# Two more input blocks in one pass, weight parts moved by transfers, and a new order behind the first 200 entries

## The chip, the cores and the metric

The kernel runs on one core of a Trainium2 chip. The metric is the device time of one execution in microseconds; smaller is better. TensorE does the matmuls into PSUM, VectorE, ScalarE and POOL (GpSimd) work elementwise, and SyncE's queue issues most of the transfers (DMA).

## The reference

Four batches of a chunked state-space recurrence (8 heads, 768 steps, head size 32, state size 16) are followed by a two-layer network with SiLU:

```
for c in range(nc):                                  # chunks of 32 steps
    cum = np.cumsum(log_a[:, :, sl], axis=-1)
    L = np.exp(cum[..., :, None] - cum[..., None, :]) * causal
    M = np.einsum('bhin,bhjn->bhij', Cc, Bc) * L
    y[:, :, sl] = M @ xc  +  einsum(Cc, state) * exp(cum)
    state = exp(sum(la)) * state + sum(Bx over the chunk)
x = y as [3072, 256]
h = x @ w_in            # [256, 2048]
g = h * 1 / (1 + exp(-h))
out = g @ w_out         # [2048, 256]
```

## The kernel before

**Tiling.** The 3072 rows are 12 units of 256 steps (unit u, three to a batch) and six pairs G of units, so a pair has 512 rows. W_in and W_out each come as eight blocks of 256 hidden columns (weights n = 0 to 7 are W_in, 8 to 15 are W_out). The weights arrive as 64-bit values and are turned into fp32 by bit operations: `lw` loads, `u` and `v` on ScalarE, `w` on VectorE, `W` on POOL.

**Two ways to multiply.** A plain fp32 matmul is recorded as two passes and is slow. The other way splits each operand into three fp32r parts, high `h`, low `l` and third `d`, and multiplies part with like part, in one pass each ("one-pass" below): three quick matmuls for one product. Pairs 1 to 5 go this way wholly. Pair 0 goes one-pass for W_in blocks 6 and 7; blocks 0 to 5 are plain fp32 (`s`, L697), and so is its whole second layer (`n1`, L761).

**The order** is written out by hand in one string, `SCHEDULE`, of 1309 entries. Each entry issues one step, and every engine and queue takes its instructions in that order. A second table, `SLOTS`, names the place of each buffer, in the order of allocation. So when a place is free again follows from these two. The entries used below:

- state part of unit u: `Lt`, `La`, `Ln`, `Lx`, `Lp` loads (SyncE); `T` transposition, `E` scans, `M` masks, `S` state steps (VectorE, L525, L512, L600, L615); `ce`, `b`, `SM`, `y`, `xh` (ScalarE; `b` is L594, `SM` L623); `B`, `C` (POOL); `g0`, `gd`, `Y` matmuls (L585, L571, L635 and L644); `x,u,0` and `x,u,1` the low and third part of the unit's output (VectorE, L651, L654)
- first layer, pair 0, plain: `s,u,j` four fp32 matmuls of 256 columns, `si` SiLU on ScalarE (L703)
- first layer, one-pass: `a,G,i` eight matmuls (high and low parts), `ax` a rescaling on ScalarE (L811), `d,G,i` four matmuls (third part), `dg` SiLU (L821); then `h` (ScalarE, L827), `l` (VectorE, L651) and `e` (VectorE, L837) split the result
- second layer: `n1,f,m` (pair 0, one fp32 matmul), `q,P,i,k,m` (three one-pass matmuls, L782), then `Va`, `Vd`, `o`, `O` for the output
- parts of weight block n: `H` high (ScalarE, L322); `lD` low and `dD` third (VectorE, L326, L330); or in their place, for W_out, `Wl` and `Wd`, which copy the scaled high part on ScalarE (L335), and `Wm` and `We`, which add the rest in place by an accumulating transfer that POOL issues (L339)

Before, W_out blocks 12 to 15 have both parts by `Wl`/`Wm` and `Wd`/`We`, blocks 10 and 11 the low part alone, and blocks 8 and 9 both parts on VectorE (`lD`, `dD`).

**What stands around the change.** On TensorE, `a,G,i` writes one of two PSUM tiles, `ga` (even i) or `gb` (odd i), which the state part uses too; `d` follows when `ax` has rescaled the tile. A unit's `Y` needs `SM` and `M`, and these need `gd` and `g0`.

Of the kernel before, what the change touches and what calls it, by code (L numbers as in the profile page):

```python
# [39 lines left out]
n1,2,0 W,11 H,10 a,1,0 Wl,10 Wm,10 n1,3,1 n1,4,0 Lt,4,1,2,0 T,4,1 x,3,1 si,1,3 S,3,3 Lp,4,0 C,4 ce,4,1 E,4,0 H,11 ax,1,0  # L40
d,1,0 E,4,1 ce,4,0 Lt,4,0,2,0 n1,5,1 Wl,11 Lx,5,1,0 Wl,13 dg,1,0 n1,4,1 T,4,0 H,8 lD,1 Ln,4,0,0,0 g0,4 lD,2 Ln,4,0,1,0
B,4 H,9 M,4,1 La,5,1,0 Wm,11 Lx,4,1,0 Wm,12 gd,4 b,4,0 lD,8 b,4,1 dD,1 n1,6,1 h,1,0 S,4,0 S,4,1 Lx,5,0,0 H,3 S,4,2
SM,4,1 n1,14,0 n1,6,0 SM,4,0 Lt,5,1,3,0 M,4,0 n1,7,0 Vn,0 Y,4 y,4,1 y,4,0 xh,4 l,1,0 n1,7,1 S,4,3 a,1,2 Vn,1 lD,9 dD,8
dD,2 H,5 a,1,1 ax,1,2 e,1,0 q,1,0,1,0 d,1,2 dD,9 q,1,0,0,1 Ln,5,0,0,0 ax,1,1 d,1,1 Wd,13 Lt,5,1,1,0 q,1,0,0,0 q,1,0,1,1
AD,3 Lt,5,1,0,0 dD,4 dg,1,2 Lt,5,0,3,0 h,1,2 a,1,4 dg,1,1 h,1,1 Lt,5,1,2,0 T,5,1 ce,5,0 Lt,5,0,2,0 ce,5,1 Lt,5,0,0,0
lD,3 a,1,3 Lp,6,0 dD,10 o,0,1,2 We,12 dD,3 x,4,1 x,4,0 l,1,2 e,1,2 ax,1,4 d,1,4 H,14 q,1,2,0,1 Ln,5,0,1,0 ax,1,3 d,1,3
l,1,1 La,5,0,0 E,5,0 dg,1,4 e,1,1 q,1,1,1,1 dg,1,3 Lt,5,0,1,0 h,1,3 q,1,1,0,1 E,5,1 T,5,0 g0,5 B,5 M,5,1 Lp,5,0 C,5 gd,5
b,5,1 lD,5 Lt,6,1,0,0 b,5,0 S,5,0 Lt,6,1,3,0 S,5,1 Wm,13 We,13 dD,5 q,1,2,1,1 La,6,0,0 q,1,2,0,0 a,1,5 Lx,6,1,0 Wl,14
ax,1,5 M,5,0 q,1,1,1,0 l,1,3 S,5,2 q,1,1,0,0 SM,5,1 dD,11 La,6,1,0 e,1,3 SM,5,0 d,1,5 h,1,4 dg,1,5 h,1,5 o,0,0,2
Lt,6,1,2,0 Lt,6,1,1,0 T,6,1 q,1,2,1,0 l,1,4 e,1,4 q,1,3,0,0 l,1,5 e,1,5 q,1,3,1,0 Wd,15 Y,5 E,6,1 Lt,6,0,1,0 y,5,0 y,5,1  # L50
xh,5 q,1,3,1,1 q,1,3,0,1 ce,6,0 Lt,6,0,0,0 a,1,7 ce,6,1 q,1,4,0,0 q,1,5,1,0 Lt,6,0,3,0 ax,1,7 q,1,4,1,0 Lt,7,1,1,0 Wm,15
We,15 d,1,7 q,1,4,1,1 dg,1,7 Lt,6,0,2,0 Wd,14 q,1,5,1,1 E,6,0 q,1,5,0,1 T,6,0 h,1,7 g0,6 Ln,6,0,1,0 x,5,0 Lx,6,0,0
Ln,6,0,0,0 B,6 La,7,1,0 M,6,1 gd,6 b,6,1 Lt,7,1,0,0 x,5,1 Wm,14 M,6,0 q,1,4,0,1 a,2,1 b,6,0 ax,2,1 a,1,6 ax,1,6 S,6,0
S,6,1 Lt,7,0,0,0 C,6 S,6,2 l,1,7 e,1,7 SM,6,1 S,6,3 d,2,1 dg,2,1 SM,6,0 q,1,7,1,0 We,14 d,1,6 dg,1,6 h,1,6 q,1,5,0,0
Lt,7,1,2,0 q,1,7,0,0 Lt,7,1,3,0 T,7,1 ce,7,1 q,1,7,0,1 Lt,8,1,1,0 Y,6 Ln,7,0,1,0 q,1,7,1,1 y,6,0 h,2,1 l,1,6 e,1,6 a,2,0
ax,2,0 q,1,6,1,0 l,2,1 e,2,1 q,1,6,1,1 y,6,1 xh,6 O,0,1,2,0,0 q,1,6,0,1 Va,1,1 x,6,1 q,1,6,0,0 d,2,0 dg,2,0 a,2,3 x,6,0
La,7,0,0 E,7,1 a,2,2 E,7,0 Va,1,0 Vd,1,0 h,2,0 l,2,0 Ln,7,0,0,0 B,7 O,0,0,2,1,0 Lp,8,0 ce,7,0 ax,2,3 q,2,1,1,0 Lx,7,1,0
d,2,3 q,2,1,0,0 Lt,7,0,3,0 Vd,1,1 Ln,8,0,0,0 ax,2,2 d,2,2 e,2,0 q,2,0,1,1 q,2,0,0,0 dg,2,3 dg,2,2 Lx,7,0,0 Lt,7,0,1,0
Lt,7,0,2,0 T,7,0 h,2,3 l,2,3 g0,7 gd,7 b,7,0 Lt,8,0,2,0 q,2,0,1,0 q,2,1,1,1 M,7,1 e,2,3 q,2,0,0,1 o,1,0,2 q,2,1,0,1
Lt,8,1,3,0 a,2,5 q,2,3,1,1 Lp,7,0 b,7,1 o,1,1,2 O,1,1,2,2,0 S,7,0 S,7,1 ax,2,5 S,7,2 O,1,0,2,3,0 Lx,8,0,0 M,7,0  # L60
q,2,3,1,0 h,2,2 SM,7,0 S,7,3 O,0,0,2,2,0 La,8,0,0 Lt,8,0,0,0 a,2,4 l,2,2 SM,7,1 ax,2,4 Lt,8,1,0,0 d,2,5 dg,2,5 h,2,5
q,2,3,0,0 d,2,4 C,7 dg,2,4 h,2,4 e,2,2 q,2,3,0,1 q,2,2,1,0 q,2,2,1,1 Lt,8,1,2,0 T,8,1 ce,8,1 O,0,1,2,3,0 ce,8,0 Y,7
y,7,0 O,1,1,2,3,0 y,7,1 q,2,2,0,0 l,2,4 e,2,4 a,2,6 l,2,5 a,2,7 O,0,1,2,1,0 O,1,1,2,0,0 e,2,5 Lx,8,1,0 Lt,8,0,1,0
# [64 lines left out]
def kernel(  # L128
# [82 lines left out]
    def f32(t):  # L211
        return t.bitcast(FP32)
# [61 lines left out]
    WF = 256  # L274
# [614 lines left out]
```

## Time and profile before

| what | value |
|---|---|
| median of 3 runs | 329.56 us (329.25 to 329.67) |
| the profiled execution's own time | 329.1 us |
| its span in the profile | 327.4 us |
| mean granted clock of TensorE | 0.999 |
| TensorE matmul records | 3064 |
| L782 (second layer, one-pass) | 400 + 80 records, 110.0 + 30.7 us busy |
| L800 (first layer, one-pass) | 504 records |
| L697 (first layer, pair 0, plain) | 96 records, 22.3 us busy |
| L761 (second layer, pair 0, plain) | 64 records, 30.0 us busy |
| transfers | 29.27 MB |

Busy times are unions over records and are given with their share of the span. A group row has line, engine, operation, output and inputs, shape, count, then busy time, the mean of one in ns, and the idle time of the engine just before with what ended it. In the chain of waits a piece has its start, its length, and the work; "x8" are eight records.

### The profile page before, as it was taken

What the parts mean: (1) busy time and instruction counts of PE and PEld (TensorE: products, weight loads), DVE (VectorE), ACT (ScalarE), POOL (GpSimd) and SP (SyncE); (2) the same over time, 40 slices, a digit from 0 to 9 for tenths busy, and PEclk for the clock granted to TensorE, in tenths of its full rate; (3) what the DMA queues carried; (4) which work ended last, traced back from release to release, by engine and by line L of the source; (5) the groups of instructions that cost most, each with busy time, mean ns of one, the idle gap of its engine ahead of it and who ended that gap; (6) DMA issues with size and microseconds to landing.
All of it is one profiled execution on the core that took longest, in us unless ns stands there. A gap on an engine that the chain in (4) does not pass through costs nothing.

```text
span 327.4 us, 7519 instructions
## 1 busy us (share of the span) xinstructions
PE 320.3 (98%) x3064; PEld 243.4 (74%) x3067; DVE 240.4 (73%) x331; ACT 209.5 (64%) x319; POOL 56.0 (17%) x74
## 2 busy tenths in 40 slices
PE   8999999999999999999999999999999999999994
PEld 3478576655687777878887778878887788888883
DVE  4998999999988965877687299665787544635553
ACT  4679978648696846583771875837775455574641
POOL 1364766326102330001200010010001000000000
PEclk9999999999999999999999999999999999999999
DMA  6979966479872663423633306514042000050003
GB/s 162 206 200 272 296 175 192 51 148 135 148 127 46 105 115 53 86 36 64 147 74 70 44 1 117 104 26 96 3 74 37 7 2 2 0 88 0 2 1 64
DMA packets 94962, 29.27 MB, mean 89 GB/s; under 512 B 80000, under 2 KB 86912, under 8 KB 94928
## 3 DMA queue, kind: packets, MB, share of 16 engines
q1 hardware_dynamic: 90960, 25.71, 37.5%
q0 software_dynamic: 1616, 2.82, 5.1%
q10 hardware_dynamic: 2352, 0.26, 0.6%
q8 instruction: 24, 0.39, 0.5%
q14 instruction: 10, 0.08, 0.1%
HBM read 22.81 MB, written 3.34 MB: 80 GB/s over the span
## 4 chain that ended last, share of the span: by engine, by line
PE 94%; SPq 2%; DMA 1%; DVE 1%; issue 1%; DVEq 0%
PE hp L782 29%; PE ga L800 18%; PE gb L800 18%; PE hp L761 9%; PE hp L697 6%; PE o_ps L782 6%; PE ga L635 2%; PE ga L585 2%; PE ga L644 2%; DMA s2k<-in_C_dram 1%; PE gb L644 1%; PE ga L571 1%; SPq L262 0%; SPq L375 0%; PE o_ps L531 0%
## 5 line engine op out<-in xcount | busy, mean ns | idle before, releaser
L782 PE MATMUL hp<-r4k,s2k 128*128 128x512 f32 x400 | 110.0, 394 | 0.0
L651 DVE SCALAR_TENSOR_TENSOR r4k<-r4k,r4k 128x1024 fp32r<-128x1024 f32 (+1 forms) x42 | 50.5, 1202 | 51.3 <-ACT r4k L827 48.2
L782 PEld LDWEIGHTS hp<-r4k,s2k 128*128 128x128 f32 x400 | 74.0, 188 | 16.4 <-issue 0.3
L800 PE MATMUL ga<-raw,s2k 128*128 128x512 f32 x240 | 62.3, 395 | 0.0
L800 PE MATMUL gb<-raw,s2k 128*128 128x512 f32 x240 | 61.1, 390 | 0.0
L800 PEld LDWEIGHTS ga<-raw,s2k 128*128 128x128 f32 x240 | 44.7, 188 | 11.4 <-ACT ga L811 0.9
L800 PEld LDWEIGHTS gb<-raw,s2k 128*128 128x128 f32 x240 | 44.8, 188 | 9.9 <-ACT gb L811 0.5
L837 DVE SCALAR_TENSOR_TENSOR r4k<-r4k,r4k 128x1024 fp32r<-128x1024 f32 x40 | 49.2, 1231 | 3.4 <-DVE r4k L651 0.9
L827 ACT ACTIVATE r4k<-r4k 128x1024 fp32r<-128x1024 f32 x40 | 42.2, 1058 | 3.2 <-issue 1.3
L811 ACT ACTIVATE ga<-ga 128x1024 f32<-128x1024 f32 x21 | 21.1, 1007 | 24.6 <-PE ga L800 23.8
L811 ACT ACTIVATE gb<-gb 128x1024 f32<-128x1024 f32 x21 | 21.2, 1009 | 17.6 <-PE gb L800 13.3
L782 PE MATMUL o_ps<-r4k,s2k 128*128 128x512 f32 x80 | 30.7, 390 | 0.0
L761 PE MATMUL hp<-r4k,s2k 128*128 128x512 f32 x64 | 30.0, 602 | 0.0
L821 ACT ACTIVATE r4k<-gb 128x1024 f32<-128x1024 f32 x21 | 21.4, 1021 | 12.4 <-PE gb L800 9.9
L520 POOL TENSOR_TENSOR BT<-bn,ab 128x256 f32<-128x256 f32 x10 | 6.7, 672 | 129.5 <-DVE ab L512 123.3
L318 POOL TENSOR_TENSOR s2k<-s2k,s2k 128x512 uint32<-128x512 uint32 (+1 forms) x19 | 23.6, 1250 | 26.4 <-DVE s2k L307 13.7
L821 ACT ACTIVATE r4k<-ga 128x1024 f32<-128x1024 f32 x21 | 21.5, 1023 | 8.4 <-PE ga L800 8.2
L512 DVE TENSOR_TENSOR_SCAN ab<-ab,diag 128x512 f32<-128x512 f32 x20 | 24.8, 1265 | 0.0
L697 PE MATMUL hp<-r4k,s2k 128*128 128x256 f32 x96 | 22.3, 382 | 0.2 <-issue 0.2
L697 PEld LDWEIGHTS hp<-r4k,s2k 128*128 128x128 f32 x96 | 18.0, 190 | 4.0 <-issue 1.4
L761 PEld LDWEIGHTS hp<-r4k,s2k 128*128 128x128 f32 x64 | 11.6, 189 | 10.5 <-issue 9.6
L782 PEld LDWEIGHTS o_ps<-r4k,s2k 128*128 128x128 f32 x80 | 15.0, 188 | 3.2
(123 smaller groups left out, 384.8 us busy)
## 6 DMA issues: line engine op xcount, KB each, us to landing
ab<-az SPq DMA_DIRECT2D x20, 256.0 KB, 4.2
raw<-in_moe_w_in_dram SPq DMA_DIRECT2D x8, 512.0 KB, 4.2
raw<-in_moe_w_out_dram SPq DMA_DIRECT2D x8, 512.0 KB, 8.0
out_dram<-r4k SPq DMA_DIRECT2D x44, 64.0 KB, 2.0
xt<-in_x_dram SPq DMA_DIRECT2D x20, 128.0 KB, 4.2
s2k<-s2k POOLq DMA_DIRECT2D x10, 256.0 KB, 3.8
pfx<-ac SPq DMA_DIRECT2D x10, 130.0 KB
bn<-in_B_dram SPq DMA_DIRECT2D x20, 64.0 KB, 5.2
```

Of the source, the lines that this page charges most:

```text
L318: nc.gpsimd.tensor_tensor(out=u[:, :, fs], in0=u[:, :, fs], in1=v[:, :, fs], op=ALU.add)
L512: nc.vector.tensor_tensor_scan(out=o, data0=src, data1=diag.rearrange("p h t -> p (h t)"), initial=0.0, op0=ALU.mult, op1=ALU.add)
L644: nc.tensor.matmul(out=y[w][32 * q:32 * q + 32, c, 64 * k:64 * k + 64], lhsT=xc[64 * c:64 * c + 64, k, h], rhs=m[64 * c:64 * c + 64, k, h] ...
L651: nc.vector.scalar_tensor_tensor(out=l, in0=f32(h), scalar=BACK, in1=y, op0=ALU.mult, op1=ALU.add)
L697: nc.tensor.matmul(out=hp[:, i], lhsT=WT[j][:, kc, 128 * i:128 * i + 128], rhs=XM()[:, 2 * kc:2 * kc + 2, u], start=(kc == 0), stop=(kc == ...
L761: nc.tensor.matmul(out=NP[m], lhsT=WT[8 + f // 2][:, f % 2, 128 * m:128 * m + 128], rhs=GT[0, f // 2][:, f % 2], start=(n == 1), stop=(n = ...
L782: nc.tensor.matmul(out=ACC[P, c], lhsT=WK[8 + i, p][:, k, 128 * m:128 * m + 128], rhs={"h": HT, "l": LT, "d": DT}[p][P, i][:, k], start=(n ...
L800: nc.tensor.matmul(out=o, lhsT=WK[j, q][:, kc, 128 * i:128 * i + 128], rhs=xs[:, 2 * kc:2 * kc + 2], start=(start and q == "h" and kc == 0 ...
L811: nc.scalar.activation(t, t, AF.Copy, scale=1.0 + Z)
L821: nc.scalar.activation(g, t, AF.Silu, scale=BACK)
L827: nc.scalar.activation(t, GT[G, i], AF.Copy, scale=-LESS * Z)
L837: nc.vector.scalar_tensor_tensor(out=DT[G, i], in0=f32(HT[G, i]), scalar=-1.0, in1=f32(LT[G, i]), op0=ALU.mult, op1=ALU.subtract)
```

## The change

- W_in blocks 2 and 3 ("three, four") of pair 0 go one-pass: `s,u,2`, `s,u,3` and their `si` (u = 0, 1) are gone; `a`, `ax`, `d`, `dg` for `0,2` and `0,3` come. They use parts of x that exist for blocks 6 and 7 already, and parts of W_in that pairs 1 to 5 use as well, so these are made earlier.
- A new step `Wc` copies the high part of a W_out block to the place of its low part by a transfer on SyncE's queue. It takes the place of `Wl` for blocks 10 to 15 and, with `Wm`, that of `lD` for blocks 8 and 9. Their third parts come by `Wd` and `We` in the place of `dD`.
- The first 200 entries of `SCHEDULE` are kept. The 1113 behind them, and the places in `SLOTS`, stand in another order. Two more steps (`ds`, `dl`) are defined and not used.

The entries that are gone and that came:

```
gone:  s,0,2 s,1,2 s,0,3 s,1,3  si,0,2 si,1,2 si,0,3 si,1,3  lD,8 dD,8 lD,9 dD,9
       Wl,10 Wl,11 Wl,12 Wl,13 Wl,14 Wl,15
came:  a,0,2 ax,0,2 d,0,2 dg,0,2  a,0,3 ax,0,3 d,0,3 dg,0,3
       Wc,8 Wc,9 Wc,10 Wc,11 Wc,12 Wc,13 Wc,14 Wc,15  Wm,8 Wm,9  Wd,8 Wd,9 We,8 We,9
```

The core of the diff, with the stretch of the order around unit 4 and the entries around block 14 and at the end:

```diff
+    def w_copy(n):
+        t = WK[n, "l"] = small(f"l{n}", [128, 2, WF], FR)
+        nc.sync.dma_start(out=f32(t).rearrange("p k f -> p (k f)"), in_=f32(WK[n, "h"]).rearrange("p k f -> p (k f)"))
...
-        "Wl": lambda n: w_part(n, "l"), "Wd": lambda n: w_part(n, "d"), "Wm": lambda n: w_more(n, "l"),
+        "Wl": lambda n: w_part(n, "l"), "Wd": lambda n: w_part(n, "d"), "Wc": w_copy, "Wm": lambda n: w_more(n, "l"),
...
-B,4 H,9 M,4,1 La,5,1,0 Wm,11 Lx,4,1,0 Wm,12 gd,4 b,4,0 lD,8 b,4,1 dD,1 n1,6,1 h,1,0 S,4,0 S,4,1 Lx,5,0,0 H,3 S,4,2
-SM,4,1 n1,14,0 n1,6,0 SM,4,0 Lt,5,1,3,0 M,4,0 n1,7,0 Vn,0 Y,4 y,4,1 y,4,0 xh,4 l,1,0 n1,7,1 S,4,3 a,1,2 Vn,1 lD,9 dD,8
...
-Ln,6,0,0,0 B,6 La,7,1,0 M,6,1 gd,6 b,6,1 Lt,7,1,0,0 x,5,1 Wm,14 M,6,0 q,1,4,0,1 a,2,1 b,6,0 ax,2,1 a,1,6 ax,1,6 S,6,0
-S,6,1 Lt,7,0,0,0 C,6 S,6,2 l,1,7 e,1,7 SM,6,1 S,6,3 d,2,1 dg,2,1 SM,6,0 q,1,7,1,0 We,14 d,1,6 dg,1,6 h,1,6 q,1,5,0,0
...
+Wc,12 E,4,0 Lt,4,0,2,0 Lt,4,0,1,0 T,4,0 g0,4 Ln,4,0,1,0 B,4 gd,4 n1,3,1 La,5,0,0 n1,5,1 b,4,0 lD,1 M,4,1 S,4,0 b,4,1
+S,4,1 S,4,2 Wc,9 Lx,5,1,0 SM,4,1 M,4,0 C,4 SM,4,0 Y,4 Lt,5,1,3,0 n1,6,1 Vn,0 Lt,5,0,1,0 y,4,0 dD,1 y,4,1 Vn,1 xh,4 Wc,10
...
+h,1,3 Wc,15 B,5 q,1,2,1,1 g0,5 Wc,11 La,6,1,0 We,9 h,1,4 Ln,6,0,1,0 M,5,1 gd,5 q,1,2,0,1 a,1,5 b,5,1 b,5,0 S,5,0
...
+Lx,7,0,0 Lt,6,0,0,0 Lt,6,0,2,0 Wd,13 q,1,1,0,1 T,6,0 q,1,4,0,0 Wd,14 Wm,15 We,15 q,1,3,1,0 g0,6 Ln,6,0,0,0 B,6 M,6,1
+h,1,7 We,13 Lx,6,0,0 gd,6 b,6,1 b,6,0 h,1,5 q,1,3,0,1 l,1,7 M,6,0 Lp,7,0 a,2,1 ax,2,1 a,1,6 ax,1,6 Lt,7,0,0,0 e,1,7
+q,1,7,1,1 Lp,6,0 S,6,0 S,6,1 S,6,2 S,6,3 x,5,1 C,6 q,1,7,0,1 d,2,1 Lt,7,0,2,0 SM,6,0 q,1,7,1,0 dg,2,1 SM,6,1 h,2,1 d,1,6
+dg,1,6 h,1,6 q,1,7,0,0 l,1,5 e,1,5 q,1,5,1,0 q,1,5,0,0 Lt,7,0,1,0 Y,6 l,2,1 y,6,0 q,1,5,0,1 Wc,14 Wm,14 We,14 a,2,0
+l,1,6 Lt,7,0,3,0 Ln,7,0,0,0 e,1,6 q,1,6,0,1 q,1,6,1,1 y,6,1 xh,6 e,2,1 x,6,0 ax,2,0 d,2,0 q,1,6,1,0 La,7,0,0 dg,2,0
...
-e,5,7 q,5,7,0,0 q,5,7,1,0 qd,5,7,1,1 Va,5,0 Vd,5,0 o,5,0,2 O,5,0,2,0,0 O,5,0,2,3,0 qh,5,6,0,1 qh,5,7,0,1 q,5,4,0,1
-Va,5,1 qd,5,6,0,1 qd,5,6,1,1 qd,5,7,0,1 Vt,5,1,1 O,5,0,2,2,0 Vt,5,1,0 ot,5,1,0 or,5,1,0 O,5,0,2,1,0 os,5,1,0,0 Vt,5,1,2
+q,5,7,1,0 q,5,5,0,0 q,5,7,0,0 O,4,0,2,1,0 Va,5,0 qh,5,6,1,1 qh,5,7,0,1 q,5,5,1,1 qd,5,7,0,1 Vd,5,0 o,5,0,2 O,5,0,2,0,0
+O,5,0,2,2,0 O,5,0,2,3,0 qd,5,6,0,1 Va,5,1 qd,5,7,1,1 O,5,0,2,1,0 Vt,5,1,1 Vt,5,1,0 ot,5,1,0 or,5,1,0 os,5,1,0,0 Vt,5,1,2
```

145 lines of the change are left out of this document (74 added, 71 removed), and 6 rows, old and new, of the table SLOTS.

## The prediction

> **What bounds the kernel now.** I read the profile's page first: busy times, the slices, the chain that ended last.
>
> ```profile
> PE 320.3 (98%) x3064; PEld 243.4 (74%) x3067; DVE 240.4 (73%) x331; ACT 209.5 (64%) x319; POOL 56.0 (17%) x74
> PE   8999999999999999999999999999999999999994
> PE 94%; SPq 2%; DMA 1%; DVE 1%; issue 1%; DVEq 0%
> ```
>
> TensorE is busy in all slices but the first and the last, and it is 94% of the chain. So a microsecond of its work taken out is a microsecond of time, if nothing else comes late in its place. What could come late is read from the busy times by stretch (the columns are PE, PEld, DVE, ACT, POOL, then granted clock, DMA share, GB/s). I cut the span where the changed order begins (31.6), at the first matmul of pair one (72.8), after the state part of unit 4 (84.2) and at the tail (320).
>
> ```profile
> 31.60:72.80 41.20, 41.20 (x428) 26.16 (x426) 38.79 (x57) 30.07 (x59) 20.50 (x20) 1.00 0.67 171
> 72.80:84.20 11.40, 11.40 (x98) 5.99 (x99) 11.25 (x17) 8.94 (x17) 5.92 (x7) 1.00 0.99 149
> 84.20:320.00 235.80, 235.80 (x2117) 189.90 (x2118) 161.99 (x193) 148.53 (x200) 16.56 (x21) 1.00 0.32 56
> 320.00:327.40 7.40, 2.93 (x14) 1.98 (x12) 2.71 (x7) 1.10 (x3) 0.00 (x0) 0.96 0.37 71
> ```
>
> TensorE never rests between 31.6 and 320. But in the first two stretches VectorE is busy 38.79 + 11.25 = 50.04 of 52.60 us: it has 2.56 us to spare, and TensorE is kept full there by slow fp32 fillers. From 84.2 on VectorE has 235.80 - 161.99 = 73.8 us to spare, and the tail is a short dependent chain. So the change is decided before 84.2: less filler is a gain only as far as VectorE keeps up.
>
> **TensorE's part.** The four calls `s,u,j` of blocks 2 and 3 (L697) go; two calls `a` and two `d` (L800) come. The chain of waits between 31 and 75 us shows both kinds as pieces.
>
> ```profile
> 47.91 1.73 PE hp L697 x8
> 51.48 1.73 PE hp L697 x8
> 58.67 1.73 PE hp L697 x8
> 63.73 1.73 PE hp L697 x8
> 46.06 1.85 PE ga L800 x8
> 49.64 0.92 PE gb L800 x4
> 60.40 0.86 PE hp L761 x2
> ```
>
> The first four pieces are the very calls that go: 4 x 1.73 = 6.92 us. What comes is 2 x (1.85 + 0.92) = 5.54 us. The sum is -1.38 us, all of it on the path. Everything else that TensorE does stays in number, the 32 fp32 matmuls of L761 among them; the last row (two records, one matmul) prices one at 0.86 us for use below.
>
> **What the other engines get.** The rows are the groups by line.
>
> ```profile
> L326 DVE TENSOR_TENSOR s2k<-s2k,s2k 128x512 fp32r<-128x512 f32 x10 | 7.5, 756 | 0.0
> L330 DVE SCALAR_TENSOR_TENSOR s2k<-s2k,s2k 128x512 fp32r<-128x512 f32 x12 | 8.4, 715 | 0.1
> L703 ACT ACTIVATE r4k<-hp 128x512 f32<-128x512 f32 x12 | 7.1, 589 | 2.6 <-PE hp L697 2.6
> L335 ACT ACTIVATE s2k<-s2k 128x512 fp32r<-128x512 f32 x10 | 6.2, 625 | 0.1
> L811 ACT ACTIVATE ga<-ga 128x1024 f32<-128x1024 f32 x21 | 21.1, 1007 | 24.6 <-PE ga L800 23.8
> L821 ACT ACTIVATE r4k<-ga 128x1024 f32<-128x1024 f32 x21 | 21.5, 1023 | 8.4 <-PE ga L800 8.2
> L339 POOL DMA_DIRECT2D s2k<-s2k x10 | 8.8, 935 | 12.9 <-DMA s2k<-s2k 5.8 <-ACT s2k L335 3.7 <-issue 3.4
> ```
>
> ScalarE: four `si` (0.589) and six `Wl` (0.625) go, two `ax` (1.007), two `dg` (1.023) and two `Wd` (0.625) come: -2.36 - 3.75 + 4.06 + 1.25 = -0.8 us. It has 41.20 - 30.07 = 11 us to spare in the first stretch, so I cost it at nothing. The price without that cover would be the 4.06 - 2.36 = 1.7 us that `ax` and `dg` put there in place of `si`.
>
> POOL: four more accumulating transfers (L339) at 0.935 = 3.7 us, on an engine 17% busy. SyncE: eight more issues. Both are costed at nothing, with the exception that the second rival names. Two of the copies wait on their queue with loads behind them: `Wc,11` stands for `H,11` of ScalarE, with the ab, B and C loads of unit 6 behind it, which the state part of unit 6 needs some ten microseconds of TensorE work later; `Wc,14` is the second rival.
>
> VectorE: the low and third parts of W_out blocks 8 and 9 leave it, 2 x 0.756 + 2 x 0.715 = 2.9 us. But all of that lay where it does not bind, or moves: what counts is VectorE's list ahead of the second product of unit 4 (`Y,4`, at about 84.2). There the new order has `lD,3`, `lD,5`, `dD,2`, `dD,3` that came later before, and has lost `lD,8` and `dD,1`: two operations more, +1.4 us (0.715 to 0.756 each). One-pass blocks need those parts of W_in early; that is their hidden price.
>
> So VectorE needs 50.04 + 1.4 = 51.4 us of work where TensorE now offers 52.60 - 1.38 = 51.2. If none of its 2.56 us of rests remained, TensorE would wait 0.2 us; if all remained, 51.4 + 2.56 - 51.2 = 2.8 us. I take 0.5, near the lower end. First, part of those rests was waiting for TensorE, which now comes sooner. Second, much of the 50.04 us is no work:
>
> ```profile
> 65.08 0.68 DVE L654 SCALAR_TENSOR_TENSOR raw<-raw,ys 128x512 fp32r<-128x512 f32 x1
> 73.21 1.30 POOL L318 TENSOR_TENSOR s2k<-s2k,s2k 128x512 uint32<-128x512 uint32 x1 [3.79 <-DVE s2k L310]
> 73.56 1.51 DVE L654 SCALAR_TENSOR_TENSOR raw<-raw,ys 128x512 fp32r<-128x512 f32 x1
> L654 DVE SCALAR_TENSOR_TENSOR r4k<-r4k,r4k 128x512 fp32r<-128x512 f32 x2 | 3.5, 1772 | 0.0
> ```
>
> In the timeline the same third part of x takes 0.68 us alone and 1.51 us when it begins under POOL's addition of L318 (73.21 to 74.51); two others of its kind average 1.772. So 1.30 us of POOL cost 0.83 us of VectorE, and with 20.50 us of POOL in the first stretch several such us stand in 38.79. What the new order meets of them is chance, in both directions.
>
> [...]
>
> **Unit 4 by itself.** Between the state products (`gd`) and `Y` runs a chain over ScalarE and VectorE. For unit 3 it is seen whole:
>
> ```profile
> 66.08 0.38 PE ga L571 x32
> 66.59 0.45 ACT L594 ACTIVATE bxs<-ga 128x128 f32<-128x128 f32 x2 [2.69 <-PE ga L571]
> 66.90 0.20 DVE L613 COPY st<-bxs 128x64 f32<-128x64 f32 x1
> 67.39 0.69 DVE L310 SCALAR_TENSOR_TENSOR s2k<-raw,s2k 128x512 uint32<-128x512 uint32 x1
> 68.00 0.28 DVE L615 SCALAR_TENSOR_TENSOR st<-st,pfx,bxs 128x64 f32<-128x64 f32 x1
> 68.31 0.64 ACT L623 ACTIVATE sm<-st,par 128x96 f32<-128x96 f32 x2 [1.28 <-DVE st L615]
> ```
>
> From `gd`'s end (66.46) to `sm` (68.95) are 2.49 us, 0.61 of them the weight operation between (67.39 to 68.00), so about 1.9. In the new order unit 4 has two matmuls of L761 between `gd,4` and `Y,4`, 2 x 0.86 = 1.72 us, where four stood. TensorE waits 0.2 us there, or up to 0.7 if `lD,1` and `M,4,1`, which stand ahead on VectorE, are late. This is part of the 0.5, not on top of it.
>
> **The sum.** The tail keeps its chain: ten matmuls follow the last one of the first output half, before eleven, and the steps after them are the same. So 329.1 us of the profiled execution (span 327.4) become 329.1 - 1.38 + 0.5 = 328.2. The median of the three runs is 329.56, 0.46 above the profiled execution; with the same difference I predict 328.7. About 0.2% (0.66 us, below 328.9 or above 330.2) is what a measurement of this kernel can tell from no change.
>
> **Rivals.** *First: VectorE sets the pace up to unit 4.* For it: 50.04 of 52.60 us, and two operations more. [...] Where the wait passes 1.38 us the gain is gone, and with all rests kept it is 2.8: 329.56 - 1.38 + 2.8 = 331.0. It decides from 1.4 of the 2.56 us of rests kept: 329.3 to 331.0. Chance 0.25, of which 0.17 above 330.2.
>
> *Second, slower: the transfers of W_out block 14 arrive late.* These rows are from the DMA issues and the timeline of POOL.
>
> ```profile
> ab<-az SPq DMA_DIRECT2D x20, 256.0 KB, 4.2
> s2k<-s2k POOLq DMA_DIRECT2D x10, 256.0 KB, 3.8
> 118.35 0.84 POOL L339 DMA_DIRECT2D s2k<-s2k  x1
> 122.28 0.88 POOL L339 DMA_DIRECT2D s2k<-s2k  x1 [2.37 <-DMA s2k<-s2k]
> ```
>
> Before, the two accumulations of block 14 were issued at 118.35 and 122.28, the second after the first had landed. Now there are three transfers in a row: `Wc,14` by SyncE, then `Wm,14`, then `We,14`. No row shows a copy on SyncE's queue; the nearest of 256 KB takes 4.2 us there and 3.8 on POOL's. The copy also stands behind four loads of units 6 and 7, the first of which waits for unit 6's transposition, and it needs the landing of `Wm,15`, whose place it takes. Three landings are 4.2 + 3.8 + 3.8 = 11.8 us, and with four issues ahead, at about 0.6 us each by the two sides' usual pace, 14.2. TensorE's work from `g0,6` to the first matmul with block 14 is some 15 us (three calls `a`, two `d` and eight `q` at the 0.23 us per matmul of the rows above, 13 us, and the small matmuls of unit 6). If the transposition comes at the last moment, a landing of 5 us instead of 3.8 already makes TensorE wait, 1 to 3 us: 329.7 to 331.7. Chance 0.17, of which 0.15 above 330.2 once the first rival's wait adds to it.
>
> *The other way:* no wait at all, and the small waits of before on ScalarE and VectorE gone too: -1.38 - 0.5, 327.7. That is the lower end of my own case, which has 0.58: 0.50 below 328.9, 0.08 within 0.2%.
>
> **How the numbers follow.** Faster 0.50; same 0.08 + 0.08 + 0.02 = 0.18; slower 0.17 + 0.15 = 0.32. The range goes from 327.5 to 331.2: it leaves out the far ends of the rivals and a larger saving. My own case alone is 327.6 to 329.3.
>
> **What would show it.** Right: L697 at 64 records instead of 96, L800 at 24 more; TensorE full from 31.6 on, and `Y,4` sooner by 0.5 to 1.4 us. Wrong by the first rival: idle TensorE before L585 or L635 ended by VectorE, before 84 us. Wrong by the second: a wait of TensorE at about 130 us ended by `s2k<-s2k`. A time above 330.2 or below 327.5 would make the sum wrong.

## The result and the profile after

| kernel | median | runs | ratio to before, 95% interval |
|---|---|---|---|
| before | 329.47 us | 20 (328.43 to 332.3) | |
| after | 331.70 us | 20 (330.81 to 333.62) | 1.0069 [1.0055, 1.0083] |

The changed kernel is slower by 2.2 us. The prediction had 328.7, so both the direction and the range (327.5 to 331.2) are missed. The profiled execution of after took 331.37 us (span 329.6), against 329.1 (327.4) before. Its busy times, TensorE's slices, and the chain that ended last:

```profile
PE 319.6 (97%) x3056; PEld 240.8 (73%) x3059; DVE 237.7 (72%) x327; ACT 209.6 (64%) x315; POOL 65.5 (20%) x78
PE   8889999999999999999999999999999999999993
PE 86%; DMA 5%; SPq 4%; ACT 2%; DVE 1%; issue 1%; DVEq 0%; ACTq 0%
```

TensorE is busy for 0.7 us less and still the span is 2.2 us longer: 10.0 us of the span are without TensorE work instead of 7.1. The same four stretches as before, with the last one up to the new end:

```profile
31.60:72.80 41.20, 41.13 (x423) 25.11 (x422) 37.87 (x60) 31.24 (x59) 24.24 (x23) 1.00 0.72 159
72.80:84.20 11.40, 11.30 (x94) 5.81 (x92) 10.02 (x18) 8.39 (x16) 5.01 (x5) 1.00 0.78 168
84.20:320.00 235.80, 235.49 (x2112) 188.26 (x2113) 161.43 (x188) 147.95 (x199) 23.58 (x26) 1.00 0.37 68
320.00:329.60 9.60, 4.20 (x20) 3.02 (x18) 2.71 (x7) 1.58 (x3) 0.00 (x0) 0.96 0.29 56
```

Three things differ. TensorE rests 0.07 + 0.10 + 0.31 us where it never rested (this counts busy records; the starts of the matmuls, used below, show more). VectorE, which I had feared, is less busy up to 84.20 (47.89 us instead of 50.04), POOL more (29.25 instead of 26.42). And the last stretch has 5.40 us without TensorE instead of 4.47.

**What TensorE does** came out as planned. In the groups, with shapes apart, L701 has 64 records, and L814 has 2 x 24 on r4k, which are pair 0's one-pass calls, 24 of them new:

```profile
L701 PE MATMUL hp<-r4k,s2k 128*128 128x256 f32 x64 | 14.6, 382 | 0.2 <-issue 0.2
L814 PE MATMUL ga<-r4k,s2k 128*128 128x512 f32 x24 | 7.5, 448 | 0.0
L814 PE MATMUL gb<-r4k,s2k 128*128 128x512 f32 x24 | 7.1, 430 | 0.0
```

**Where it waits.** Two places of the chain of waits, around `g0,3` and before `Y,4`:

```profile
66.88 1.03 ACT r4k L835
67.90 0.34 ACT bxs L598 x2
68.29 0.33 PE ga L589 x2
...
83.67 0.70 ACT sm L627 x2
84.46 0.27 PE ga L639 x2
```

`dg,0,3` (1.03 us on ScalarE) stands ahead of `b,3`, and `b,3` ahead of `g0,3`: the second of the two added `dg` is itself the chain. At `Y,4` TensorE rests 0.36 us, from the end of its filler to the end of `SM,4`. Further on the chain leaves TensorE in places where it did not before. Behind unit 8, a load of ab for unit 10, the scan of it and `x,8,0` on VectorE, and then `y,9` on ScalarE stand ahead of `a,3,7`:

```profile
205.26 4.96 DMA ab<-az
210.25 1.22 DVE ab L516
211.48 0.59 DVE raw L655
212.15 0.40 ACT ys L676
```

**The end.** The last pieces of the chain, before and then after:

```profile
321.30 0.92 PE o_ps L782 x4
...
323.62 0.42 DVE s2k L747
```

```profile
322.57 0.92 PE o_ps L796 x4
...
324.89 0.42 DVE s2k L751
```

TensorE's last W_out matmul ends at 322.22 and 323.49, the last VectorE copy at 324.04 and 325.31: the steps between last equally long. But from that copy to the end of the span are 3.36 us before and 4.29 after. Only transfers of output run there, and in their queues over the last five microseconds (324.60 to 329.60) one line is new; before's last five (322.40 to 327.40) have nothing but q1 and q10, which carry the output.

```profile
...
q14 instruction: 1, 0.01, 0.6%
```

A packet of instructions for an engine is loaded among the last output rows. Both kernels have ten such packets; before's last one falls between 312 and 320 us, after's beyond 324.

**The sum.** In the profiles the first matmul run that both kernels share after the start begins at 26.41 us before and 27.15 after, though the first 200 entries are the same. In repeats it began at 27.84 (before) and 27.28 (after), so that is the execution's, not the change's. Beyond it, the content of TensorE is -1.46 us, all of it ahead of `Y,4`. With the starts taken off, `Y,4` comes at 57.31 and 57.22 us in the two profiles of after (the second is the first experiment's) and at 57.72 and 57.49 in those of before: 0.3 us sooner on average, so waits of 1.1 us have been added up to there. From `Y,4` to the last W_out matmul, where both have the same content, after takes 0.9 us more (238.9 on average, before 238.0), and the end takes 1.0 us more (6.15 and 6.26, before 5.17 and 5.16). That gives -1.46 + 1.1 + 0.9 + 1.0, or about +1.6, and 1.6 is what the whole profiles differ by, starts taken off (300.7 and 302.3 us on average). About 0.6 us of the 2.2 are not in these profiles; the runs below say what they can be.

The 1.1 us up to `Y,4` fall in these places of the first pair: about 0.43 at `Y,4`, 0.15 ahead of `a,0,2` (its tile is held by `dg,0,6`), 0.07 at `Y,2`, and 0.34 at `g0,3`. Of the last, 0.14 is a wait. The other 0.20 is the price of a plain filler that stands between two groups of small matmuls: from start to start, a first pass behind such a group takes 0.53 us and a last one ahead of it 0.52, where the others take 0.43, in both kernels, and the new order has one such place more.

### The profile page after: what moved, and what is told of

Its sections match the earlier page's. It is cut to its first block, busy times and chain, and to the rows that moved or that the text cites. A ratio compares the mean times of both kernels' runs of the same rounds, so it can differ in the third digit from the quotient of the medians.

```text
span 329.6 us, 7508 instructions
## 1 busy us (share of the span) xinstructions
PE 319.6 (97%) x3056; PEld 240.8 (73%) x3059; DVE 237.7 (72%) x327; ACT 209.6 (64%) x315; POOL 65.5 (20%) x78
## 4 chain that ended last, share of the span: by engine, by line
PE 86%; DMA 5%; SPq 4%; ACT 2%; DVE 1%; issue 1%; DVEq 0%; ACTq 0%
PE hp L796 27%; PE gb L814 18%; PE ga L814 17%; PE hp L775 6%; PE o_ps L796 5%; PE hp L701 4%; DMA s2k<-in_B_dram 2%; PE ga L589 2%; PE ga L639 2%; DMA ab<-az 2%; PE ga L648 1%; DMA s2k<-s2k 1%; PE gb L648 1%; PE ga L575 1%; SPq L269 1%; SPq L262 1%
## 5 line engine op out<-in xcount | busy, mean ns | idle before, releaser
L796 PEld LDWEIGHTS hp<-r4k,s2k 128*128 128x128 f32 x400 | 74.0, 188 | 16.3 <-issue 0.2
L655 DVE SCALAR_TENSOR_TENSOR r4k<-r4k,r4k 128x1024 fp32r<-128x1024 f32 (+1 forms) x42 | 51.5, 1227 | 37.4 <-ACT r4k L841 36.6
L814 PE MATMUL ga<-raw,s2k 128*128 128x512 f32 x240 | 62.9, 397 | 0.0
L814 PE MATMUL gb<-raw,s2k 128*128 128x512 f32 x240 | 61.5, 392 | 0.1
L814 PEld LDWEIGHTS ga<-raw,s2k 128*128 128x128 f32 x240 | 44.4, 188 | 12.0 <-ACT ga L825 1.7
L814 PEld LDWEIGHTS gb<-raw,s2k 128*128 128x128 f32 x240 | 44.4, 188 | 10.9 <-ACT ys L676 0.5
L825 ACT ACTIVATE ga<-ga 128x1024 f32<-128x1024 f32 x22 | 22.2, 1009 | 18.9 <-PE ga L814 18.9
L835 ACT ACTIVATE r4k<-gb 128x1024 f32<-128x1024 f32 x22 | 22.6, 1026 | 18.4 <-PE gb L814 12.4
L318 POOL TENSOR_TENSOR s2k<-s2k,s2k 128x512 uint32<-128x512 uint32 (+1 forms) x19 | 26.4, 1393 | 22.5 <-DVE s2k L310 10.3
L835 ACT ACTIVATE r4k<-ga 128x1024 f32<-128x1024 f32 x22 | 22.5, 1024 | 10.8 <-PE ga L814 9.5
L516 DVE TENSOR_TENSOR_SCAN ab<-ab,diag 128x512 f32<-128x512 f32 x20 | 23.7, 1206 | 2.3 <-DMA ab<-az 2.3
L524 POOL TENSOR_TENSOR BT<-bn,ab 128x256 f32<-128x256 f32 x10 | 9.6, 955 | 69.0 <-PE ga L648 18.2
L555 POOL TENSOR_TENSOR cw<-ct,pfx 128x256 f32<-128x256 f32 x9 | 8.3, 920 | 62.1 <-DMA xt<-in_x_dram 25.8
L604 DVE TENSOR_TENSOR ab<-gb,ab 128x512 f32<-128x512 f32 x12 | 8.2, 686 | 14.0 <-PE gb L589 8.8
L775 PEld LDWEIGHTS hp<-r4k,s2k 128*128 128x128 f32 x64 | 11.5, 189 | 9.0 <-issue 7.4
```

The costliest lines, as they stand in the source:

```text
L318: nc.gpsimd.tensor_tensor(out=u[:, :, fs], in0=u[:, :, fs], in1=v[:, :, fs], op=ALU.add)
L516: nc.vector.tensor_tensor_scan(out=o, data0=src, data1=diag.rearrange("p h t -> p (h t)"), initial=0.0, op0=ALU.mult, op1=ALU.add)
L524: nc.gpsimd.tensor_tensor(out=BT[u][:, ks], in0=bn[u][:, ks], in1=E[u][:, ks, :, Q - 1:Q].to_broadcast([128, n, H, N]), op=ALU.mult)
L655: nc.vector.scalar_tensor_tensor(out=l, in0=f32(h), scalar=BACK, in1=y, op0=ALU.mult, op1=ALU.add)
L775: nc.tensor.matmul(out=NP[m], lhsT=WT[8 + f // 2][:, f % 2, 128 * m:128 * m + 128], rhs=GT[0, f // 2][:, f % 2], start=(n == 1), stop=(n = ...
L796: nc.tensor.matmul(out=ACC[P, c], lhsT=WK[8 + i, p][:, k, 128 * m:128 * m + 128], rhs={"h": HT, "l": LT, "d": DT}[p][P, i][:, k], start=(n ...
```

## The experiments

Each median has before's median of the same set of runs beside it. New order entries are shown by their neighbours.

**Both kernels again, in profile and time.** No edit; the same order of steps, executed again.

> The changed kernel as it is, for a second profile. In its first profile TensorE stood 0.74 us longer than in the kernel before up to the first call s of block 1, in a stretch whose order is the same in both, and about 0.9 us longer between TensorE's last matmul and the end. If these are the change's own, both come again, to 0.2 us; if the first is the luck of one execution, it goes (the wait before tp,1, which a load of B ends, 1.1 us in the first profile, is then near 0.4), and the tail's 0.9 us stays, since its order did change.

> The kernel before as it is, for a second profile. If the start's difference is luck, its start varies by some tenths of a us, too; the tail (last matmul to the end of the last transfer) should repeat the 3.5 us of the first profile to 0.2 us.

After: 331.23 us, span 329.5; before: 330.07, span 328.3. Between 28 us and the tail, the wait at `Y,4` (L639) stands in both profiles of after, and one at `a,3,7` (L814) is listed in the second alone; before had neither in either profile.

```profile
PE ga L639 <- ACT sm L627: 0.4, 1, 0.4
PE gb L814 <- ACT ys L676: 0.2, 1, 0.2
```

So the wait at `Y,4` belongs to the order, and the start does not.

**After, with the copies on ScalarE.**

```diff
-Wc,8 Wc,9 Wc,10 Wc,11 Wc,12 Wc,13 Wc,14 Wc,15
+Wl,8 Wl,9 Wl,10 Wl,11 Wl,12 Wl,13 Wl,14 Wl,15      (each in its place)
```

> The changed kernel with its eight copies on SyncE given back to ScalarE at the same places of the order (an activation of 0.63 us each), the accumulations on POOL kept. Theory transfers (the copies on SyncE's queue and what they collide with cost the time): 1 us or more faster than the changed kernel, about 330.5. Theory order (the places of the new order and the tail cost it, whoever copies): the same as the changed kernel to 0.4 us, 331.3 to 332.1. Theory VectorE (the one-pass blocks ask too early for its parts): the same, too.

341.14 us against 329.10, 1.0367 [1.0328, 1.0405]. Waits of TensorE:

```profile
PE hp L796 <- DMA s2k<-s2k: 3.4, 2, 2.2
PE o_ps L796 <- DMA s2k<-s2k: 3.1, 1, 3.1
```

ScalarE has time enough for eight copies of 0.62 us, but its order puts them late: block 14's copy ran at 133.76 us, and its two accumulations behind it. The granted clock was 0.91 between 140 and 160 us, after these waits. At these places of the order ScalarE's copies cost 9.4 us more than SyncE's (331.70); none of my theories expected that.

**Before, with the copies on SyncE's queue.**

```diff
-Wl,10 Wl,11 Wl,12 Wl,13 Wl,14 Wl,15
+Wc,10 Wc,11 Wc,12 Wc,13 Wc,14 Wc,15                (each in its place)
```

> The kernel before with its six ScalarE copies of W_out blocks 10 to 15 given to SyncE at the same places of the order, nothing else. Theory transfers: slower by 0.7 us or more, above 330.2. Theory order and theory VectorE: the kernel before's time to 0.4 us, 329.1 to 329.9.

341.54 us against 329.10, 1.0378 [1.0337, 1.0419]. A copy at the head of SyncE's queue waits for its `H` on ScalarE, and the loads of the next units wait behind it. The chain of waits has loads of ab and x in it, and TensorE waits for what is made of B:

```profile
61.28 3.92 DMA ab<-az
85.80 4.18 DMA xt<-in_x_dram
```

```profile
PE ga L575 <- POOL BT L524: 3.1, 2, 2.9
```

The clock was 0.78 between 84.2 and 100 us. Swapping the way of copying costs 12.4 us in before's order and 9.4 in after's, neither of which was made for it, so neither run isolates the copy itself.

**More matmuls behind the first output half** ("the moved end" below; 13 instead of 10, where before had 11).

```diff
-q,5,4,0,1 qh,5,6,0,1 q,5,6,1,0 qd,5,6,1,1 ... l,5,7 qh,5,7,1,1 ... Va,5,0 qh,5,6,1,1 qh,5,7,0,1 q,5,5,1,1
+q,5,4,0,1 q,5,6,1,0 ... l,5,7 ... q,5,5,1,0 qh,5,7,1,1 ... Va,5,0 qh,5,6,1,1 qh,5,7,0,1 qh,5,6,0,1 q,5,5,1,1 qd,5,6,1,1
```

> The changed kernel with three entries of its last ones moved: qh,5,6,0,1 and qd,5,6,1,1 (three matmuls of the second output half) go behind Va,5,0, so that 13 matmuls, and not 10, follow the last one of the first half; qh,5,7,1,1 changes places with q,5,5,1,0. Theory order (the tail's 1.0 us is the cover that the new order gives up): the last stores start 0.68 us sooner against TensorE's end, the stretch from TensorE's last matmul of W_out to the end goes from 6.1 to 5.2 us or less, and the time to 330.7 or less (331.7 - 1.0). Rival (the last transfers simply took longer in these executions, or the chain over TensorE alone sets the end): no change beyond 0.3 us.

330.92 us against 329.50, 1.0053 [1.0024, 1.0082]. There is more TensorE work behind `Va,5,0`, and the first half's rows go out 0.68 us sooner, but the end hardly shortened: the last copy ends at 324.60 of a span of 328.8, 4.2 us after 4.29. My theory of too little cover for the first half's stores is false. The median is 0.5 to 0.8 us below after's, by ratio or by time, with intervals that overlap; the end doesn't explain that. The DMA queues from 323.80 to 328.80:

```profile
...
q14 instruction: 1, 0.01, 0.7%
```

The packet of instructions is still there.

**The moved end and eight small VectorE operations.** Eight memsets of a scratch tile, ahead of `a,4,6`, add eight instructions to VectorE and nothing to the output. The first kernel below has them on top of the last one, the second alone on after.

```diff
+    def c_zero(): nc.vector.memset(tiny, 0.0)
-q,4,5,1,1 a,4,6
+q,4,5,1,1 zd zd zd zd zd zd zd zd a,4,6
```

> The kernel with the moved tail, and eight memsets of one column on VectorE among its work of pair 4, which are no part of the computation. In the kernels with the new order an 8 KB transfer of the queue of instructions falls 3.3 us behind TensorE's last matmul of W_out, among the last rows of the output, in the kernel before 8 us ahead of them; 446 to 448 of VectorE's instructions are through at that time in both. Theory instruction load (VectorE has 15 instructions fewer, so that its last load of code falls into the tail, and one of the 16 engines is late with its rows): the transfer falls before TensorE's end, the last row lands 3.5 us behind it, not 4.2, and the time goes from 330.9 to 330.3. Rival (another engine's load, or the rows are late by themselves): the transfer stays where it is or the last row still lands at 4.1 or later.

> The changed kernel with the eight memsets of one column on VectorE among its work of pair 4 (they are no part of the computation), and nothing moved. Theory instruction load (the last load of code, which the new order lets fall into the tail, holds up one of 16 engines and the end with it): 0.5 to 0.9 us faster than the changed kernel in spite of eight instructions more, 330.8 to 331.2, and the stretch from TensorE's last matmul of W_out to the end goes from 6.1 to 6.3 us to 5.4 or less. Rival (the tail's length is that of the later stores, as the prediction's chain would have it): 6.1 us stay, and so does the time.

With the moved end: 330.27 against 329.57, 1.0027 [1.0002, 1.0053]. Alone: 331.03 against 329.79, 1.0045 [1.0021, 1.0068]. From the last copy to the end of the span are 328.7 - 325.34 = 3.36 us in the first and 330.9 - 327.34 = 3.56 in the second; the packet loads sooner and is no longer among the last five microseconds. The end of the first kernel:

```profile
322.37 1.15 PE o_ps L799 x5
324.92 0.42 DVE s2k L754
```

So eight idle operations give back the loss of the end. They are on VectorE alone, so it is VectorE's instructions that move this load: in the second kernel from about +2 us to -2.5 us, counted from the end of the last transposing matmul. The count of instructions fits. With all of VectorE's instructions in the trace, those too that the page leaves out, after has 450 and before 465, and the last load begins when VectorE has begun 445 to 450 of them, in every profile. The other engines stand at very different counts then: ScalarE at 382 to 416, SyncE at 282 to 303. With 15 instructions fewer in all, that point is among the last.

| VectorE instructions | last load begins, from the end of the last transposing matmul | end of the span from there |
|---|---|---|
| 450 (after, three profiles, and five variants) | +1.85 to +2.2 us | +4.57 to +4.90 us |
| 451 (one kernel) | -0.1 | +4.08 |
| 453 (two kernels) | -0.1, +0.2 | +3.85, +4.31 |
| 458 to 462 (six kernels) | -2.5 to -8.1 | +3.42 to +3.99 |
| 465 (before, two profiles) | -8.4, -8.1 | +3.80, +3.79 |
| 466 (before with the copies on SyncE) | -15.8 | +3.43 |

The second kernel's profile (span 330.9) was slow for another reason, both third parts that come by transfer:

```profile
PE o_ps L799 <- DMA s2k<-s2k: 1.1, 1, 1.1
PE hp L799 <- DMA s2k<-s2k: 0.4, 1, 0.4
```

```profile
99.82 0.94 POOL BT L527
100.76 6.32 DMA s2k<-s2k
...
128.01 3.32 DMA s2k<-s2k
...
131.86 4.83 DMA s2k<-s2k
```

Block 9's accumulation stands behind `B,5` on POOL and took 6.32 us to land; block 14's two are those of the second rival.

**The state part's surroundings.**

```diff
-n1,7,1 n1,6,0 E,4,1      -dD,0 lD,4 d,1,0      -n1,5,0 H,15 w,9,0
+gd,4 n1,6,0 n1,3,1       +M,4,0 lD,4 C,4       +SM,3,1 H,15 w,11,0
```

> The changed kernel with three entries moved before unit 4's output: n1,6,0 from ahead of g0,4 to behind gd,4 (three fp32 matmuls of cover between gd,4 and Y,4, not two), lD,4 behind M,4,0 on VectorE, H,15 behind SM,3,1 on ScalarE. Theory order: the waits of 0.43 us before Y,4 and 0.34 us before g0,3 go, nothing takes their place: 0.5 to 0.8 us faster than the changed kernel. Theory VectorE (it sets the pace there): what is taken from one wait comes back at the next, less than 0.3 us.

331.77 against 329.50, 1.0055 [1.0030, 1.0080]. The wait of `Y,4` is gone and stands at `g0,4` (0.39 us by the chain). The list of waits ends it with `lD` on VectorE at 79.66 us; `dg,1,0` on ScalarE ended at 79.65, and the second of the mended versions below tells which of them counts. The wait at `g0,3` stays, and block 9's third part is late:

```profile
PE hp L796 <- DMA s2k<-s2k: 0.8, 1, 0.8
```

**All these moves, and fillers at three later waits** (`x,8,0` ahead of `E,10,1`; `q,4,3,1,1` ahead of `a,4,4`; `q,4,6,0,0` ahead of `a,5,1`).

> The changed kernel with the moves of the two runs above and three small ones: x,8,0 ahead of E,10,1 on VectorE, q,4,3,1,1 ahead of a,4,4 and q,4,6,0,0 ahead of a,5,1 on TensorE. Theory order: the sum, 1.0 + 0.77 + 0.5 = 2.2 us faster than the changed kernel, 329.4, about the kernel before's time or just under it. Theory transfers or VectorE: at least 1 us of the loss stays, 330.5 or more.

332.00 against 329.50, 1.0065 [1.0041, 1.0089]. The wait at `a,3,7` went (0.34 to 0), one of 0.5 us before `d,4,4` came in its place: the filler moved had been the cover of that one.

**The plain `s` of blocks 2 and 3 back,** at the places of the one-pass calls, with `lD` and `dD` of these blocks behind `Y,4`. This undoes the first part of the change alone.

> The changed kernel with blocks 2 and 3 of the first pair in fp32 again (the four calls s,u,j and si,u,j where the d calls stood, lD and dD of blocks 2 and 3 behind Y,4), the new order and the transfers kept. TensorE gets 1.38 us more. Theory order (the one-pass blocks are worth their 1.38 us, the loss is of the places): 1.0 to 1.6 us slower than the changed kernel, 332.7 to 333.3. Theory VectorE (the early parts of W_in cost what TensorE saves): the same as the changed kernel to 0.4 us, or faster, since its waits before g0,3 and Y,4 go.

337.05 against 329.50, 1.0224 [1.0179, 1.0269]. Block 9's third part landed 2.1 us late, and the windows around that wait show what followed it:

```profile
111.00:114.00 3.00, 0.95 (x5) 0.52 (x4) 2.97 (x4) 0.94 (x1) 0.85 (x1) 1.00 1.16 213
114.00:117.00 3.00, 3.00 (x9) 2.38 (x8) 2.01 (x3) 0.41 (x1) 0.00 (x0) 0.54 0.79 178
```

With 0.95 us of work in 3 us, TensorE was granted 0.54 of its clock in the next three, and nine matmuls ran where thirteen would fit at 0.227 us. That the wait brought the lower clock is my reading of their order in time. The run is confounded by this clock and by a start that was slow, too. All six runs (336.07 to 340.07 us) lie far above the 332.7 to 333.3 that I expected. So the price of the plain calls against the one-pass blocks was never measured by itself; that rival stays open.

**`We,9` sooner** (behind `Wm,12`, ahead of `B,5`).

> The changed kernel with one entry moved: We,9 (the accumulation that makes the third part of W_out block 9) from behind B,5 to behind Wm,12 on POOL, some 8 us sooner. In four kernels with the new order it landed between 4.0 us ahead of and 0.8 us behind the first matmul that reads it (q,1,1), and behind it by 2.2 us in a fifth, where TensorE's clock fell, too. Theory transfers late (block 9 stands where the second rival put block 14): the accumulation lands before 98 us in the profile, the timed runs above 332 us become rare, and the median goes from 331.7 to 331.2 or less. Rival (order alone): the median stays within 0.3 us of 331.7.

330.92 against 329.57, 1.0056 [1.0030, 1.0082], runs 329.86 to 333.55, four of the twelve still above 332. Block 9 landed at 93.2 us, 13 us ahead of its first use. But this profile (331.1 us of span) shows block 14 late. First the timeline of POOL in after, where all was in time, then this kernel's:

```profile
125.03 0.88 POOL L343 DMA_DIRECT2D s2k<-s2k  x1 [0.80 <-DMA s2k<-s2k]
128.88 0.86 POOL L343 DMA_DIRECT2D s2k<-s2k  x1 [2.97 <-ACT sm L627]
```

```profile
127.64 0.89 POOL L343 DMA_DIRECT2D s2k<-s2k  x1 [3.72 <-DMA s2k<-s2k]
131.50 0.86 POOL L343 DMA_DIRECT2D s2k<-s2k  x1 [2.97 <-ACT r4k L841]
```

```profile
PE o_ps L796 <- DMA s2k<-s2k: 1.5, 1, 1.5
```

The copy landed 2.6 us later, and TensorE waited 1.5 us at block 14. This is the second rival, at its place and in its size, in an execution of a kernel that leaves block 14's entries as they are.

**`We,9`, `Wc,14` and `Wm,14` sooner** (the copy behind `Ln,6,0,0,0`, the accumulation behind `We,13`).

> The changed kernel with the transfers of W_out blocks 9 and 14 sooner (We,9 behind Wm,12, Wc,14 behind Ln,6,0,0,0, Wm,14 behind We,13), and nothing else. Theory transfers late (block 14, as the second rival had it, and block 9 in some executions only): no run waits for either, the spread of the runs (2.8 us in the changed kernel) falls to under 1.8 us, the median to 331.0 or less. Rival (the slower ones among the runs have another cause, such as the start): spread and median stay within 0.3 us of the changed kernel's.

330.70 against 329.79, 1.0031 [1.0014, 1.0049], runs 329.77 to 331.99. No wait for either block. But VectorE has one instruction more (451), its last load began 2 us sooner, and about 0.8 us of the gain are the end's. The spread of 2.2 us did not shrink as expected, so how much the late transfers cost on average is not told by this run.

**Blocks 8 and 9 by VectorE again** (`lD,8 dD,8` behind `dD,1`, `lD,9 dD,9` behind `We,12`; their four copies and accumulations gone).

> The changed kernel with the low and third parts of W_out blocks 8 and 9 made by VectorE again (lD and dD of block 8 behind dD,1, of block 9 where We,12 stands) and not by transfers; the six copies on SyncE stay. Theory transfers late: no wait for block 9 is left, and the median is 331.2 or less. Theory VectorE (it has no room behind Y,4 either): slower than the changed kernel, 332.5 or more, with new waits of TensorE between 85 and 100 us.

330.32 against 329.57, 1.0025 [1.0005, 1.0045]. About 1.4 us less than after, 0.9 of it the end (453 VectorE instructions). VectorE had room for 2.9 us of work there.

**The mended versions.** The first joins the moved end, the eight operations, the sooner transfers, fillers at `g0,3`, `a,3,7` and `a,5,1`; the second also moves `lD,4` and `lD,5` behind `Y,4` and `n1,6,0` behind `gd,4`; the third adds blocks 8 and 9 by VectorE to the second.

> The changed kernel with the moved tail, the eight memsets, We,9 sooner, Wc,14 behind Ln,6,0,0,0 and Wm,14 behind We,13 (block 14 some 5 us sooner), x,8,0 ahead of E,10,1, q,4,6,0,0 ahead of a,5,1, and n1,14,1 ahead of g0,3. If the causes found add up: 331.7 - 0.5 (late transfers) - 0.9 (tail) - 0.7 (waits before g0,3, a,3,7 and a,5,1) = 329.6, the kernel before's time. If they do not, 330.5 or more.

> The version with moved tail, memsets and sooner transfers of blocks 9 and 14, and besides lD,4 and lD,5 moved from ahead of Y,4 to behind it on VectorE (just ahead of dD,4 and dD,5), and n1,6,0 from ahead of g0,4 to behind gd,4. The list ahead of Y,4 is two operations shorter, as in the kernel before. Theory VectorE pace (the first rival: its list, not the place of the fillers, sets g0,4 and Y,4): where the filler alone was moved the wait went from Y,4 (0.43 us) to g0,4 (0.39 us); now both are under 0.15 us, and the time is 0.4 us under that version's 330.36. Rival (the chain gd, b, S, SM sets Y,4 whatever VectorE has ahead): a wait of 0.3 us or more before g0,4 or Y,4, and no gain.

> The version of the run before with W_out blocks 8 and 9 made by VectorE again. If late transfers, the load in the tail, VectorE's list ahead of Y,4 and the small waits are the whole loss, what is left is TensorE's 1.38 us less some tenths: 328.5 to 329.3, faster than the kernel before. If not, it stays at 329.6 or above.

330.36 against 329.57, 1.0022 [0.9998, 1.0046]; 330.21 against 329.79, 1.0026 [1.0003, 1.0049]; 331.63 against 329.79, 1.0074 [1.0048, 1.0099]. I had expected 329.6 of the first and 328.5 to 329.3 of the third. The second takes two operations off VectorE's list ahead of `Y,4`, as the first rival would have it, and gains nothing: the wait at `g0,3` went, and about 0.5 us came at `Y,3`. Its chain at `g0,4`, which now is the one that waits 0.3 us:

```profile
78.28 0.95 PE ga L817 x4
...
79.31 1.03 ACT r4k L838
80.39 0.33 PE ga L592 x2
```

It is `d,1,0`, its `dg` on ScalarE, and `g0,4` in the tile that `dg` reads, with no filler between. In the third VectorE does run out of room, and then the waits bear its name:

```profile
PE hp L799 <- DVE r4k L854: 1.1, 1, 1.1
PE ga L592 <- DVE bh L532: 1.1, 1, 1.1
```

**After once more, and a mix.** The mix has blocks 8 and 9 by VectorE, the moved end with the eight operations, `Wc,14` and `Wm,14` sooner, and fillers at `a,3,7` and `a,5,1`; `lD,4` and `lD,5` stay where after has them.

> The changed kernel as it is, timed beside the mixture below on one chip, with a third profile. Theory transfers late: W_out block 14 lands near the first matmul that reads it (margin of its third part 2.3 to 2.8 us in the first two profiles, none in two kernels that leave it where it is), so that among the runs some are 1 us and more above the others; the median is 331.3 to 332.0. Rival (the loss is the same in every run): the runs lie within 1 us of each other.

> The changed kernel with the parts of W_out blocks 8 and 9 made by VectorE (lD, dD), Wc,14 and Wm,14 sooner, the moved tail, the eight memsets, x,8,0 ahead of E,10,1 and q,4,6,0,0 ahead of a,5,1; VectorE's list ahead of Y,4 as in the changed kernel. If the late transfers, the load in the tail and the small waits are what the change lost beside the fillers: 329.6 to 330.0, within 0.2% of the kernel before, but not under it, since the waits before g0,3 and Y,4 (0.8 us) stay.

After: 332.11 against 329.31, 1.0075 [1.0046, 1.0103]; its profile lost its time at the start, and block 14 had 3.0 us to spare. The mix: 329.47 against 329.31, 1.0012 [0.9998, 1.0026], ten of twelve runs within 1.1 us. It is as fast as before, not faster, though it keeps the one-pass blocks and what they save; the waits at `g0,3` and `Y,4` are still there. No version tried beats the kernel before.

## Why the prediction was wrong, step by step

**TensorE's part was right.** 64 and 24 records as forecast, -1.46 us by the traces for -1.38.

**The sum.** Of -1.38 + 0.5 the first term held. In place of 0.5 stand waits of 1.1 us up to `Y,4`, 0.9 us behind it and 1.0 us at the end, the last two of which the sum put at nothing; 0.6 us more lie outside the profiles. (The sum has a slip, too: the lower end of the first rival, with 1.4 us of rests kept, is 329.56 - 1.38 + 1.6 = 329.8, not 329.3.)

**VectorE's pace: the mechanism was wrong, and the term too small.** I put 51.4 us of work against 51.2 on offer and took 0.5 us of wait. VectorE was busy for 47.89 us, with four more operations than before, and between 28 and 322 us no wait of after bears its name. Taking operations off its list only moved a wait (the second mended version), so the first rival is refuted for this change; it appears when more is added (the third).

Why the same kind of work took less time, the traces tell for the most part. The prediction's third part of 1.77 us, which stood beside POOL's work, is this in after:

```profile
L658 DVE SCALAR_TENSOR_TENSOR r4k<-r4k,r4k 128x512 fp32r<-128x512 f32 x2 | 1.4, 678 | 0.0
```

Before, both began while POOL was adding (33.15 to 36.52 us); here each began ahead of POOL's addition (33.75 against 33.90, 39.15 against 39.76). Operations that no elementwise work of POOL overlaps take the same time in both kernels (this third part 0.68 us, a scan 1.20, a state step 0.28). Added up from about 31 us to `Y,4`, those that it overlaps were 10.8 us longer than that in both profiles of before, and 6.3, 7.0 and 7.9 in three of after. Without this excess VectorE's work is 45.2 to 45.3 us before and 46.0 to 46.2 after, so the added operations did cost 0.7 to 1.0. This excess, of which the prediction said that what the new order meets is chance, was 3 to 4.5 us smaller in after, and the difference goes with the order, since it repeats in each kernel's profiles. No run moved POOL's work alone, so that POOL is the cause rests on this comparison.

**ScalarE "costed at nothing" is the step that failed in its place.** By throughput it was right: 39.63 us busy of 52.60. But `ax` and `dg` hold a PSUM tile and stand in ScalarE's order ahead of `b` and `SM`. The price of 1.7 us "without that cover" was in the text; 1.1 us of waits was the measure, of which 0.43 at `Y,4` is as the unit 4 step had it (0.2 to 0.7), and at `g0,3` the chain is one `dg`. `Y,4` came 0.4 us sooner than before when the starts are taken off (84.46 - 27.15 against 84.13 - 26.41), and 0.27 in the second pair, short of the 0.5 to 1.4 given. That ScalarE is the cause is read from what ended these waits; no run took `ax` and `dg` away by themselves.

**The rest of the order was not looked at.** The sum has no term between unit 5 and the end, and 0.9 us were lost there, in waits and pauses of at most 0.5. I had taken the 73.8 us that VectorE has to spare as a reason. What I now think counts is the filler at each `g0`, `Y` and `a`, since 1100 entries stand in another order; but no run isolates the 0.9 us by such fillers.

**"The tail keeps its chain" failed.** The chain of engines did stay; the end behind it grew by 0.9 us by the load of VectorE's instructions. That eight added VectorE operations take it away is shown on two kernels. The trace names the queue as instruction loads; that this one is VectorE's follows from those two kernels and from the count above.

**The second rival was right in its mechanism and not in after's own three profiles.** Accumulations of the changed kernel took longer, as the DMA issues have it (3.8 before):

```profile
s2k<-s2k POOLq DMA_DIRECT2D x14, 256.0 KB, 4.8
```

Block 14's third part had 8.8 to 9.8 us to spare before and 2.2 to 3.1 in after's profiles; in two profiles of variants with the same entries it came late, for 1.1 and 1.5 us. Block 9 I had not named: 0.6 to 4.0 us to spare in after, late in four variants by 0.2 to 2.1 us. That such executions make the 0.6 us that the profiles do not hold is plausible; what share is theirs and what the start's stays open.

## What to carry to other kernels

Count what a saving takes from the cover, place by place: here 1.4 us of slow matmuls were also the filler of several short chains, and an engine with 25% of its time free still stood, by the latency of one instruction, at the end of waits on the path. Where work is moved to transfers, the margin of the last landing at its first use is the number to watch, over several executions; and when an engine loses instructions, look whether its instruction loads have moved to where nothing hides them.

## What the hardware showed that I had not expected

- Instructions are loaded during the run, in packets of 8 KB on a queue of their own (q14, ten packets in both kernels). One packet among the last output rows cost 0.7 to 0.9 us (4.29 us from the last copy to the end, against 3.56 and 3.36 in the two kernels with eight operations more), though its own share of the DMA engines in the last five microseconds is 0.6%.
- An accumulating transfer of 256 KB within SBUF landed in 3.3 to 5.9 us, with a median of 3.8, where ten of them ran (before), and in 3.3 to 6.6, with a median of 4.8, where fourteen ran beside eight copies (after).
- The same VectorE operation, a third part of x, took 0.68 us by itself and 1.77 beside elementwise work of POOL. In the stretch up to `Y,4` such excess added up to 10.8 us before and 6.3 to 7.9 after, so it differed by microseconds between the two orders.
- A wait of 2.1 us for one transfer was followed by three microseconds at 0.54 of the clock, in which nine matmuls took 3.00 us; behind one of 1.5 us they took 0.23 each from the second on.
